# Sigmoid attention and a token mixer on one core: every transpose of q, k and x behind the first group in four 64x64 tiles

## The chip, the cores and the metric

The kernel runs on one core of one Trainium2 chip. The metric is the device time of one execution in microseconds. A core has five engines that run side by side and meet only through semaphores: TensorE (PE in the profile; its weight loads are shown apart as PEld), VectorE (DVE), ScalarE (ACT), GpSimd (POOL) and SyncE (SP), which here only issues DMAs. TensorE writes into PSUM, here eight banks of 2 KB for each of 128 partitions; another engine has to copy a result out of PSUM before the bank can be written anew.

## The reference

Inputs are q, k and v of shape (8, 12, 448, 64), and three weights, all f32; the output is (8, 448, 768) in f32.

```python
scores = q @ k.T / sqrt(64) - log(448)
attn   = sigmoid(scores)                    # no softmax: each element by itself
x      = (attn @ v), heads side by side     # (8, 448, 768)
wq, wk = x @ w_q, x @ w_k                   # 768 -> 64
W_tok  = wq @ wk.T / sqrt(64)               # 448 x 448 for each batch
out    = relu(W_tok @ x) @ w_out
```

The kernel computes W_tok @ x as wq @ (wk.T @ x), so the 448 x 448 matrix of the second part is never made.

## The kernel before, in words

**Work units.** Four heads of one batch are a group; there are 8 batches of 3 groups, 24 groups n = 0 to 23. Rows of a head are split as 448 = 7 x 64. For each group the kernel loads q, k and v (448 KB each, SP, L180) into one ring of five buffers, and POOL casts each to bf16 (L199). q and k have two cast buffers each, v three. A cast of q or k waits for the transposes of the group two before it, and a load waits for the cast that frees its ring buffer. So SP, POOL and PE are tied in a ring.

**Steps.** PE's work is written out by hand as a string of letters, PLAN (L125 to L152), and the loop at L649 turns each letter into one step, on all engines in that order:

- S: scores of one 64-row block, 4 matmuls of 64x64 tiles (L263) into a pair of banks, then one ACT sigmoid of 128x896 (L268). There are 168.
- P: attn @ v, 4 matmuls (L281). Seven P of a group add up in one pair of banks, which DVE copies out (L290).
- q and k, or a and b: transposes of one group's q or k (`tr`, L225). Letters q and k use `transposes`: 28 transposes of 64x64, in the four 64x64 tiles of the array (L213). Letters a and b use `transposes_whole`: 7 transposes of 128x128 in the whole array (L221). Both forms use one pair of banks for q and k together, and one DVE copy (L251 or L246).
- x or X: transposes of one group's part of x for the mixer (`tr_x`, L295). x: 32 transposes of 64x64 (L321), into a pair of banks. X: 8 of 128x128 (L304), into a single bank. One DVE copy follows either (L334 or L309).
- W, N, U, M: the steps of the mixer (L345, L361, L376, L399 or L411), and O: the output product (L481 for batches 0, 1, 6 and 7 in the whole array, L446 for the others in 64x64 tiles), with copies on DVE or ACT and stores from SP. Lower-case m, u and o put the copy on ACT.
- F: one matmul of zeros (L651).

The eight PSUM banks are four pairs, and they are handed out in the order in which they were released, as the program is built:

```python
    free2 = [0, 1, 2, 3]
    def bank2():
        n = free2.pop(0)
    def bank1():
        if halves:
            n, b = halves.pop(0)
        else:
            n, b = free2.pop(0), 0
            halves.append((n, 1))
```

`bank2` takes a pair, `bank1` a single bank: the free half of a pair that is already split, or the first half of a new one. `release` puts a pair at the end of the list. A step waits on PE until the copy of the step that had its banks before is done; the instructions behind it on PE wait too, since PE works in order. W keeps a single bank over six steps, P a pair over seven, and O a single bank or a pair over two or four.

In PLAN the first group's q and k are transposed ahead of the loop in the whole array (L631 to L641 and K), which stays so. Of the 23 pairs of q and k steps behind it, 11 are a and b (groups 1, 2, 4, 5, 7, 8, 9, 10, 13, 14 and 15); of the 24 x steps, 9 are X (groups 0, 1, 3, 4, 5, 6, 8, 10 and 16).

Of the kernel before, what the change touches and what calls it, by code (L numbers as in the profile page):

```python
# [16 lines left out]
def kernel(  # L17
# [94 lines left out]
    def xt(u, j):  # L112
# [11 lines left out]

    PLAN = (  # L125
        "FFFSSSFFFFFKFSSaFbSFSPPPP",
        "SSPPaPSbSSFqkSFFSFa",
        "SXSbSPPPPSPPFSPSabPSPPP",
        "SPPSPWWSXSxWSWWWSPPNSPPP",
        "SqPkSSPaSbSUSXSPPPM",  # L130
        "SPPPSPSabSaSbaSbSPPPMP",
        "SPPPSWXWSMSWXWSSWoWOSqkP",
        "SPPPSPPPSoOSSSoOONSO",
# [15 lines left out]
        "SUSoSoMOSOSPPPPxSPPPS",  # L149
        "PPPmPPMPPWWoWWWWoOxxNoOUOOoOMmMoOOoooOooOOOOooOooO",  # L150
    )
    PLAN = "".join(PLAN)  # L152
    KIND = ["a"] + [t for t in PLAN if t in "qac"]

    ld = {}
# [492 lines left out]

    for t in PLAN:  # L649
        if t == "F":  # L650
# [28 lines left out]
        elif kind == "M":  # L679
            u, x = divmod(c, NC // 2)  # L680
# [43 lines left out]
```

## Time and profile before

| | |
|---|---|
| timed runs, median of 3 | 204.12 us (203.43 to 205.49) |
| span of the profiled execution, first to last instruction | 200.3 us |
| PE busy | 187.9 us (94%), 3,948 matmuls and transposes |
| PEld busy | 122.1 us, 3,950 weight loads |
| ACT busy | 170.3 us (85%), of it 157.0 us the 168 sigmoids |
| DVE busy | 125.0 us (62%) |
| POOL busy | 82.1 us (41%) |
| DMA | 49.73 MB, mean 248 GB/s |
| granted TensorE clock, mean | 0.998 |

The profiled execution is one execution apart from the timed ones. Its records begin and end with its span, so no time around it can be read from it; the timed median lies 3.8 us above the span, and that difference is taken as fixed.

The page gives busy times, a picture of the span in 40 slices of 5 us, and the chain of work that ended last. Matmul records have modelled ends, which overlap the next start, so a busy PE can still hide short waits; how long a step holds PE is read from the start of its first matmul to the start of the next step's.

### The profile page before, as it was taken

The numbers are of one execution on the slowest core, as the hardware profiler recorded it, in microseconds if no ns is written. First come the engines' busy times: TensorE is split into PE (matmuls) and PEld (weight loads), VectorE is DVE, ScalarE is ACT, GpSimd is POOL, SyncE is SP. The second block draws the span as 40 slices with busy tenths as digits, with TensorE's granted clock in tenths as the row PEclk, the third lists the DMA queues.
The fourth block names the chain that finished last, engine by engine and source line by source line (L and its number), as shares of the span: only waits on it lengthen the run. The fifth ranks groups of instructions, "written<-read, shape, count | busy, mean of one in ns | idle before, by whom it ended". The sixth has DMA issues, their size and how long they took to land.

```text
span 200.3 us, 8999 instructions
## 1 busy us (share of the span) xinstructions
PE 187.9 (94%) x3948; PEld 122.1 (61%) x3950; DVE 125.0 (62%) x165; ACT 170.3 (85%) x194; POOL 82.1 (41%) x101
## 2 busy tenths in 40 slices
PE   8995998898999999999999999999999999999990
PEld 7452564455455655665557667778678869665560
DVE  3234375667755877846786856667787774774520
ACT  4798899798989999999889799999899989975520
POOL 2467777677677647558136320305061110000000
PEclk9999999999999999999999999999999999999999
DMA  5999999999999999899999983388704443332575
GB/s 174 317 351 374 292 361 324 357 358 322 356 352 348 367 389 315 293 320 339 285 318 352 338 301 104 86 242 208 256 17 99 105 109 81 84 79 49 142 211 154
DMA packets 29799, 49.73 MB, mean 248 GB/s; under 512 B 3904, under 2 KB 26560, under 8 KB 29760
## 3 DMA queue, kind: packets, MB, share of 16 engines
q1 hardware_dynamic: 29040, 47.78, 74.2%
q10 hardware_dynamic: 720, 1.38, 1.9%
q8 instruction: 31, 0.51, 1.0%
q14 instruction: 8, 0.07, 0.1%
HBM read 38.14 MB, written 11.01 MB: 245 GB/s over the span
## 4 chain that ended last, share of the span: by engine, by line
PE 61%; DMA 26%; POOL 5%; ACT 2%; issue 1%; SPq 1%; ACTq 1%; DVE 1%; POOLq 0%; DVEq 0%
PE banks L446 14%; PE banks L263 12%; PE banks L281 11%; PE banks L481 8%; DMA k<-in_k_dram 8%; DMA q<-in_q_dram 8%; DMA v<-in_v_dram 6%; DMA out_dram<-o 5%; PE banks L345 4%; POOL q L199 2%; PE banks L376 2%; PE banks L221 2%; PE banks L321 2%; PE banks L213 2%; ACT at L268 2%
## 5 line engine op out<-in xcount | busy, mean ns | idle before, releaser
L268 ACT ACTIVATE at<-banks,bias_t 128x896 bf16<-128x896 f32 x168 | 157.0, 1012 | 11.8 <-PE banks L263 9.5
L263 PE MATMUL banks<-qk 64*64 64x448 bf16 x672 | 62.4, 360 | 1.2 <-ACT at L268 0.5
L281 PE MATMUL banks<-at,v 64*64 64x448 bf16 x672 | 45.9, 350 | 0.5 <-issue 0.5
L263 PEld LDWEIGHTS <-qk 64*64 64x64 bf16 x672 | 24.9, 105 | 21.2 <-issue 13.7
L446 PE MATMUL banks<-wout,mx 64*64 64x384 bf16 x672 | 36.3, 323 | 0.0
L199 POOL CAST v<-v 128x896 bf16<-128x896 f32 x24 | 22.4, 933 | 30.5 <-PE banks L281 21.1
L290 DVE CAST xt<-banks 128x896 bf16<-128x896 f32 x23 | 25.1, 1090 | 12.6 <-PE banks L281 12.6
L481 PE MATMUL banks<-wout,mx 128*128 128x384 bf16 (+1 forms) x174 | 31.1, 321 | 0.0
L199 POOL CAST k<-k 128x896 bf16<-128x896 f32 x23 | 21.4, 932 | 18.2 <-PE banks L213 10.5
L281 PEld LDWEIGHTS <-v 64*64 64x64 bf16 x672 | 23.1, 106 | 6.6 <-issue 0.3
L387 DVE TENSOR_SCALAR mx<-banks 128x1024 bf16<-128x1024 f32 (+2 forms) x22 | 22.7, 1044 | 6.9 <-PE banks L411 3.5
L199 POOL CAST q<-q 128x896 bf16<-128x896 f32 x23 | 21.4, 932 | 9.3 <-DMA q<-in_q_dram 5.6
L446 PEld LDWEIGHTS <-mx 64*64 64x64 bf16 x672 | 22.6, 107 | 4.0
L481 PEld LDWEIGHTS <-mx 128*128 128x128 bf16 x174 | 15.6, 98 | 12.4 <-issue 3.8
L251 DVE COPY qk<-banks 128x1792 bf16<-128x1792 bf16 x12 | 13.1, 1090 | 8.7 <-PE banks L213 7.2
L511 DVE COPY o<-banks 128x384 f32<-128x384 f32 x18 | 10.0, 556 | 9.1 <-PE banks L481 8.6
L246 DVE COPY qk<-banks 128x1792 bf16<-128x1792 bf16 x11 | 12.0, 1091 | 5.5 <-PE banks L221 5.3
L455 DVE COPY o<-banks 128x768 f32<-128x768 f32 x14 | 13.4, 955 | 2.4 <-PE banks L446 2.3
L334 DVE COPY xn<-banks 128x1024 bf16<-128x1024 bf16 (+1 forms) x15 | 9.7, 654 | 5.3 <-PE banks L321 5.2
L345 PE MATMUL banks<-xt,wqk 128*128 128x448 bf16 x48 | 12.6, 354 | 0.3 <-DVE o L511 0.3
L603 POOL CAST wout<-w 128x768 bf16<-128x768 f32 x12 | 9.9, 827 | 5.8 <-DMA w<-in_moe_w_out_dram 5.6
L511 ACT COPY o<-banks 128x384 f32<-128x384 f32 x9 | 4.4, 484 | 7.7 <-PE banks L481 6.9
(60 smaller groups left out, 158.5 us busy)
## 6 DMA issues: line engine op xcount, KB each, us to landing
q<-in_q_dram SPq DMA_DIRECT2D x24, 448.0 KB, 5.8
v<-in_v_dram SPq DMA_DIRECT2D x24, 448.0 KB, 5.3
k<-in_k_dram SPq DMA_DIRECT2D x23, 448.0 KB, 6.0
out_dram<-o SPq DMA_DIRECT2D x48, 192.0 KB, 3.2
w<-in_moe_w_out_dram SPq DMA_DIRECT2D x11, 384.0 KB, 4.8
out_dram<-o ACTq DMA_DIRECT2D x6, 192.0 KB, 3.2
w<-in_moe_w_out_dram SPq DMA_DIRECT2D x2, 192.0 KB, 6.0
k<-in_k_dram SPq DMA_DIRECT2D x1, 256.0 KB, 5.2
```

The source lines that it names most:

```text
L199: eng.tensor_copy(out=t16.rearrange("p i b d -> p b i d"), in_=ld.pop((nm, n)).rearrange("p b (i d) -> p b i d", i=NI),)
L251: nc.vector.tensor_copy(out=qk[n].rearrange("p t h i n -> p t h (i n)"), in_=ps[:, :, 0 : 2 * S].rearrange("p h (t x) -> p t h x", t=2),)
L263: nc.tensor.matmul(sc[HALF[h], g, 0:S], qk[n][HALF[g], 1, h, i, :], qk[n][HALF[g], 0, h].rearrange("p i n -> p (i n)"), start=True, stop=True,
L268: nc.scalar.activation(at, sc[:, :, 0:S], ACTF.Sigmoid, bias=bias_t, scale=attn_scale)
L281: nc.tensor.matmul(ps[HALF[g], h, 0:S], ld["v16", n][HALF[h], i, g, :], ats[n, i][HALF[h], g, :], start=(i == 0), stop=(i == NI - 1),)
L290: nc.vector.tensor_copy(out=xt(u, j)[:, :, 0:S], in_=ps[:, :, 0:S])
L345: nc.tensor.matmul(ps, wqk16[:, c, :], xt(u, c // 2)[:, c % 2, 0:S], start=(c == 0), stop=(c == NC - 1),)
L387: nc.vector.tensor_scalar(dst, ps, moe_scale, 0.0, ALU.mult, ALU.max)
L446: nc.tensor.matmul(ps[HALF[x], y, 0:NB], mx[HALF[y], u, b, 64 * (i - 3 * y) : 64 * (i - 3 * y) + 64], wout16[HALF[y], slot(y, b), x * NB : ...
L455: COPY["s" if act else "v"](out=o, in_=ps[:, :, 0:NB])
L481: nc.tensor.matmul(ps, mxs[w][:, 2 * S * c + m * P : 2 * S * c + (m + 1) * P], wout16[:, c, w0:w1], start=(c == 0), stop=(c == NC - 1),)
L511: COPY["s" if act else "v"](out=o[:, nb * NB : (nb + 1) * NB], in_=ps)
```

## The change

One line is added behind the plan: each a becomes q, each b becomes k and each X becomes x. The sequence of steps is the same.

```diff
-    PLAN = "".join(PLAN)
+    PLAN = "".join(PLAN).replace("a", "q").replace("b", "k").replace("X", "x")
     KIND = ["a"] + [t for t in PLAN if t in "qac"]
```

KIND is used only to find a letter c, which occurs in neither plan. What a step does follows from its letter, in `tr`:

```python
        if kind in "ab":
            transposes_whole(ps[:, t], t16, slice(0, NI))
        else:
            transposes(ps[:, :, t * S : (t + 1) * S], t16, slice(0, NI))
```

and in `tr_x`, which for X takes `bank1()` and 8 whole transposes, and otherwise `bank2()` and four times 8 transposes of 64x64. PE's program grows from 7,902 to 9,258 instructions (28 transposes in place of 7 for a q or a k, 32 in place of 8 for an x, each with its weight load). On DVE the copies L246 and L309 become L251 and L334, one for one. ACT, POOL and SP have the same instructions in the same order.

## The prediction

> **What bounds the kernel now.** First the page: the busy slices and the chain.
>
> ```profile
> PE   8995998898999999999999999999999999999990
> ...
> ACT  4798899798989999999889799999899989975520
> ...
> DMA  5999999999999999899999983388704443332575
> ...
> PE 61%; DMA 26%; POOL 5%; ACT 2%; issue 1%; SPq 1%; ACTq 1%; DVE 1%; POOLq 0%; DVEq 0%
> ```
>
> PE ends the chain most, yet the DMA engines stand at 9 for the first 24 slices, and ACT is at 8 or 9 until 175 us. So I ask for busy times by stretch (start:end length, then PE, PEld, DVE, ACT, POOL, clock, DMA share, GB/s).
>
> ```profile
> 20.00:55.00 35.00, 32.15 (x567) 19.17 (x567) 22.68 (x26) 32.24 (x36) 25.89 (x32) 1.00 0.99 338
> 55.00:66.00 11.00, 10.68 (x204) 5.62 (x204) 6.38 (x10) 9.92 (x12) 8.15 (x11) 1.00 1.01 353
> 66.00:82.00 16.00, 15.97 (x304) 9.89 (x301) 12.86 (x15) 15.57 (x17) 8.70 (x10) 1.00 0.99 349
> 82.00:100.00 18.00, 17.72 (x392) 10.44 (x380) 11.82 (x16) 17.17 (x20) 10.66 (x12) 1.00 0.94 311
> ```
>
> Up to 55 us the loads set the pace: DMA share 0.99, and PE waits for casts that waited for a load, last 0.66 us at 55.29 for group 11's k. From 66 to 82 us PE has no idle time, but ACT has 0.43 us in 16: two bounds within 3%. Behind 142 us DMA is at 0.39 and PE is busy throughout.
>
> Which steps change where, from PE's timeline: eight of the 11 pairs stand before 47 us, the others at 66.0, 68.9 and 78.4; the X at 20.9, 28.8, 38.9, 49.7, 51.3, 74.1, 87.5, 99.0 and 142.8.
>
> **What a step costs PE.** The timeline has both forms (start, length, instruction).
>
> ```profile
> 63.22 0.38 PE L263 MATMUL banks<-qk 64*64 64x448 bf16 x4
> 63.43 0.39 PE L213 MATMUL banks<-ident,q 64*64 64x64 bf16 x28
> 63.65 0.43 PE L213 MATMUL banks<-ident,k 64*64 64x64 bf16 x28
> 63.91 0.38 PE L263 MATMUL banks<-qk 64*64 64x448 bf16 x4
> ...
> 68.63 0.36 PE L263 MATMUL banks<-qk 64*64 64x448 bf16 x4
> 68.93 0.56 PE L221 MATMUL banks<-ident,q 128*128 128x128 bf16 x7
> 69.33 0.55 PE L221 MATMUL banks<-ident,k 128*128 128x128 bf16 x7
> 69.81 0.38 PE L263 MATMUL banks<-qk 64*64 64x448 bf16 x4
> ```
>
> Read starts: 28 small transposes take 0.22 us, 7 whole ones 0.40 (68.93 to 69.33). Where the array changes form there is more: S takes 0.19 us before a step of its own form and 0.31 before a whole one (+0.12); the second whole seven takes 0.49 (+0.09). So a pair between S steps falls by 2 x 0.18 + 0.21 = 0.57 us. An X goes from 0.445 (8 whole, groups of the trace) to about 0.26 (32 small); between two W, which are whole, it loses the gain to two new changes of form (0.445 to 0.475). Sum: 22 x 0.18 + 9 x 0.185 = 5.6 us, and 11 fewer visits to the whole form x 0.21 = 2.4: PE sheds **8.0 us**, 6.2 of them before 55 us.
>
> [...]
>
> **Part 1, before 55 us: 0 (-0.4 to 0).** Faster PE work does not bring the next load sooner. The cover is the load stream; the DMA share leaves at most 3% of the ten busiest us before 50, some 0.3 us. PE merely waits longer for the same casts. The four stretches in which PE waits there (0.7 at 33.9, 1.0 at 35.8, 1.2 from 41.6 to 45.7, 0.8 at 54.2) also absorb what parts 3 and 5 cost this early.
>
> **Part 2, 55 to 74 us: -0.2 (-0.5 to 0).** Two pairs save 1.15 us on PE, but ACT takes only what it idles: 0.15 us at 65.8 and 0.21 at 73.47. S steps here start 0.09 to 0.5 us after their banks come free, so PE runs into ACT instead.
>
> **Part 3, other banks for x.** X fits into the free half of W's pair; x takes a whole pair, the oldest released. I followed the list of free pairs through both plans: 38 steps get other banks. Look at the X at 74.14.
>
> ```profile
> 72.98 0.57 PE L263 MATMUL banks<-qk 64*64 64x448 bf16 x8
> ...
> 73.77 0.54 PE L345 MATMUL banks<-xt,wqk 128*128 128x448 bf16 x2
> 74.14 0.61 PE L304 MATMUL banks<-ident,xt 128*128 128x128 bf16 x8
> 74.68 0.38 PE L263 MATMUL banks<-qk 64*64 64x448 bf16 x4
> 75.00 0.93 PE L345 MATMUL banks<-xt,wqk 128*128 128x448 bf16 x4
> ...
> 73.47 2.80 ACT L268 ACTIVATE at<-banks,bias_t 128x896 bf16<-128x896 f32 x3 [0.21 <-PE banks L263]
> ```
>
> At 72.98 PE issues S 67 and S 68; ACT runs them from 73.47 to 75.4. Before, the next S (69) took a pair free since 74.48. After, x waits for sigmoid 67 (74.48 instead of 74.14) and S 69 for sigmoid 68: 75.4 instead of 74.68. From an S to its sigmoid it is 0.49 us (72.98 to 73.47), so ACT stands idle 0.55 us, and, as four W (0.86) and a change of form stand between S 69 and S 70, another 0.2. **+0.8 us** (0.4 to 0.8; ACT has nothing in reserve there). The pair saved at 78.4 returns none: S 74 started 0.12 us after its bank came free. The X at 87.5 costs nothing: an O copy fills ACT (0.48 at 88.68). At 99.0 an S then waits for x's own DVE copy: **+0.2** (0 to 0.25). At 142.8 x waits for the DVE copy of P, which ends at 143.09: 0.37 + 0.26 + a form change of 0.12 against 0.445, **+0.3** (0 to 0.4). The cases at 28.8, 49.7 and 51.3 (up to 0.7 us) are in part 1's cover; without it they would cost 1.2.
>
> **Part 4, DVE: 0.** L246 and L251 take 1091 and 1090 ns, L309 and L334 688 and 690.
>
> **Part 5, more instructions: +0.5 (0 to 3).** The code itself comes by DMA.
>
> ```profile
> q8 instruction: 31, 0.51, 1.0%
> ...
> 113.51 0.57 PE L281 MATMUL banks<-at,v 64*64 64x448 bf16 x7
> 114.57 0.35 PE L281 MATMUL banks<-at,v 64*64 64x448 bf16 x1 [0.49 <-issue]
> ```
>
> 31 packets for 7,898 PE records: one packet is 255 instructions, and the records between packets agree. At 113.51 PE stops amid a step, one matmul short, for no semaphore; the packet records show one packet from 112.01 to 112.98, and the count there is a multiple of 256 if PE's sequencer runs 73 ahead. With that offset, the sequencer's entry into a block is followed by the end of the next block's packet after 1.7 to 5.2 us until 120 us (median 3.6), and after 1.3 to 3.1 later; first use was at least 1.1 us behind that end, and 1.6 where PE stopped. So while the DMA engines are full a block of 256 should last about 5 us. Before, blocks there last 4.8 to 9.4. A tiled pair has 112 instructions in 0.45 us, and with the new counts laid on the old times blocks shrink to 4.2 to 4.7 for most of 21 to 49 us, and to 3.7, 4.1, 3.5 and 4.5 at 63.0, 66.7, 78.4 and 87.8. The early ones are in part 1's cover. Of the late four I take 0.5 us in all: none if the short delays hold (1.7 and 2.4 at 57 and 73), 3 if the long ones do (3.6 to 4.4 at 80 to 91).
>
> [...]
>
> **Sum:** 0 - 0.2 + 0.8 + 0.2 + 0.3 + 0 + 0.5 = +1.6 us on the span of 200.3; with the 3.8 us between span and median, 204.12 + 1.6 = **205.7 us**.
>
> **Rivals.**
>
> *PE's saving comes through* (faster). It does if the loads have slack and ACT's gaps close: ACT idles 3.7 us from 20 to 60 and 0.7 us from 60 to 90; half of the first and most of the second give about -2.5 us, 201.6. For it: the chain names PE most, and the DMA rate reaches 389 GB/s in one slice against 338 here. Against: casts wait for loads up to 55 us. It decides whether group 11's k (cast at 54.30) comes over 1.5 us sooner.
>
> *Code comes too late* (slower). Place: the blocks at 63.0 to 92 us; price up to 1 us each, plus early ones beyond the 3.8 us cover; it decides if crossing to use exceeds 4.5 us in them. +4, 208.
>
> *Everything is hidden:* PE's lead swallows part 3 and part 5, 204.1. For it: PE waits 3.8 us before 55. Against: ACT is at 97% where part 3 falls.
>
> That the tiled transposes do not run at 7.8 ns beside full DMA is not a rival: 12 pairs already do, at 17.7, 54.2 and 63.4 too.
>
> **Chances.** Forecast 0.50 (204.4 to 207.0), code late 0.18 (207 to 210), hidden 0.18 (203.6 to 204.4), saving 0.14 (199 to 203.3). About 1% (2 us) is what a measurement of this kernel can tell, with 203.43 to 205.49 for one kernel. Over 206.16 lie all of the second and a third of the first: slower 0.34; under 202.08 about 0.09; within 1% 0.57. Range 202.3 to 208.4: a third of the saving and some half of the late code are in, and what is left out is under 2 in 10.
>
> **What would show it.** Right: 0.22 us from q to k at all pairs; k 11 cast within 0.5 us of 54.3; an ACT idle of about 0.5 us before S 69; ACT at 97% around 66 to 82. Late code: PE idle on "issue" in mid-step, and 36 or 37 packets on q8. Wrong: sigmoids 1 us or more ahead by 55 us, or PE idle of several us at x steps.

## The result, and the profile after

The changed kernel takes 212.28 us (median of 3, 211.28 to 214.16) against 204.12: a ratio of 1.041 (95% interval 1.031 to 1.052). The forecast was 205.7 with a range of 202.3 to 208.4. It is slower, by more than the range allows. The rival that came true is the one of the code that comes too late, but it cost 8.2 us where I gave it 4, and the time lies above that rival's own 207 to 210 too.

The profiled execution after has a span of 210.5 us. Later runs list each execution's span beside its time, and the time lies 1.8 to 1.9 us above the span, not 3.8: the profiled execution of before, at 200.3, was 2 us faster than its own median. In what follows the two traces are compared span with span (+10.2 us), and times with times (+8.2 us).

The page of the changed kernel, the same slices (with the clock) and the chain:

```profile
PE   7968869776799978999899999999989999999991
...
ACT  4796979895699978999787989999969899994521
...
PEclk9997999996999999999999999999999999999998
DMA  6999999999999999369996896457823333530585
...
PE 75%; issue 7%; ACT 6%; DMA 6%; DVE 1%; ACTq 1%; POOL 1%; SPq 1%; DVEq 0%
...
q8 instruction: 36, 0.59, 1.1%
```

"issue", time in which PE waited for nothing that the profile shows, went from 1% to 7% of the chain; DMA went from 26% to 6%. PE is less busy in the first 16 slices, and the granted clock has slices at 7 and 6. Five more packets of code were loaded, 36.

Busy time by stretch, after, with the columns of the prediction (stretch and its length in us; PE with its matmul records in brackets, weight loads, DVE, ACT, POOL; granted clock; DMA share; GB/s):

```profile
20.00:55.00 35.00, 26.36 (x816) 16.95 (x812) 18.31 (x20) 28.15 (x30) 24.27 (x29) 0.93 1.00 330
55.00:66.00 11.00, 10.69 (x226) 6.03 (x222) 7.30 (x9) 9.86 (x11) 7.75 (x9) 1.00 0.99 348
66.00:82.00 16.00, 13.83 (x357) 7.54 (x356) 10.47 (x13) 13.94 (x16) 9.09 (x10) 1.00 0.99 337
82.00:100.00 18.00, 17.25 (x459) 10.01 (x443) 12.15 (x16) 17.05 (x20) 8.40 (x10) 1.00 0.71 245
```

From 20 to 55 us PE is busy for 26.4 us and ACT for 28.2, where both had 32.2 before; from 66 to 82 PE fell from 16.0 to 13.8 and ACT from 15.6 to 13.9. Not only PE: all that follows PE got less work in the same time.

What PE's idle time waited for, before (cause: us in total, times, longest), two lines of the table of waits of PE alone:

```profile
PE banks L263 <- ACT at L268: 0.5, 1, 0.5
PE banks L281 <- issue: 0.5, 1, 0.5
```

and after:

```profile
PE banks L263 <- issue: 4.0, 3, 2.2
PE banks L213 <- issue: 2.6, 3, 1.6
PE banks L263 <- ACT at L268: 2.5, 7, 0.5
PE banks L281 <- issue: 1.7, 2, 1.0
...
PE banks L321 <- ACT at L268: 1.3, 4, 0.5
...
PE banks L321 <- issue: 0.9, 1, 0.9
PE banks L481 <- issue: 0.8, 1, 0.8
```

Idle on "issue" rose from 0.5 to 10.0 us over ten stops, on five kinds of line: it is no step of its own that is slow. Waiting for ACT, that is for banks, rose from 0.5 to 3.8.

PE's timeline at the largest stop, after:

```profile
46.67 0.38 PE L263 MATMUL banks<-qk 64*64 64x448 bf16 x3 [0.30 <-ACT at L268]
49.29 0.53 PE L263 MATMUL banks<-qk 64*64 64x448 bf16 x1 [2.24 <-issue]
49.29 0.74 PE L213 MATMUL banks<-ident,k 64*64 64x64 bf16 x25
```

S is four matmuls; three are issued at 46.67 and the fourth 2.6 us later, with no semaphore between them. Count PE's records, and add 73 as in the prediction. Of the gaps of over 0.45 us between two neighbours, ten then sit where the count is 7 modulo 256, in blocks 2, 4, 6, 7, 8, 9, 12, 13, 17 and 28: 12.8 us from start to start. So a block of code is 256 of PE's records in this trace. I call these stops at a block's end. At each of them the packet of the next block had ended 1.2 to 1.6 us before PE went on. The trace of before has one such stop, of 0.8 us at 113.7, the one that the prediction shows; a gap of 0.5 us at 18.5 has nearly the same count, but the last packet had ended 5.3 us before it was over.

How late each S step starts after against before gives the course of the loss (us, by the number of the S step):

| S step | start before | later after | what stands there |
|---|---|---|---|
| 18 | 24.2 | 0.5 | |
| 21 | 26.8 | 1.9 | stop at 25.7 |
| 39 | 44.2 | 2.5 | stops at 36.4 and 41.8, partly caught up |
| 48 | 54.0 | 6.4 | stops at 46.7 and 53.3 |
| 51 | 57.4 | 5.4 | wait for group 11's cast, shorter than before |
| 66 | 71.6 | 7.0 | stop at 76.4 |
| 69 | 74.7 | 7.9 | bank waits at x and S |
| 90 | 95.3 | 8.9 | stop at 100.6 |
| 138 | 145.1 | 9.2 | bank wait at x |
| 141 | 148.6 | 10.2 | stop at 155.1 |
| 165 | 173.9 | 10.2 | |

Not all of the 5.4 us up to 57 us need be the change's. The run with only the last three pairs changed (below) has the code of before up to 60 us, and no stop at a block's end there; in its trace S 51 starts 2.7 us later than in the trace of before all the same, since casts and loads came later.

The steps themselves cost what was forecast. PE's timeline of the pair of group 12, after, and then the case that was priced bank by bank, S 67 to S 69:

```profile
60.40 0.38 PE L263 MATMUL banks<-qk 64*64 64x448 bf16 x4
60.61 0.39 PE L213 MATMUL banks<-ident,q 64*64 64x64 bf16 x28
60.83 0.43 PE L213 MATMUL banks<-ident,k 64*64 64x64 bf16 x28
...
80.14 0.57 PE L263 MATMUL banks<-qk 64*64 64x448 bf16 x8
...
81.69 0.45 PE L321 MATMUL banks<-ident,xt 64*64 64x64 bf16 x32 [0.23 <-ACT at L268]
82.59 0.38 PE L263 MATMUL banks<-qk 64*64 64x448 bf16 x4 [0.45 <-ACT at L268]
```

From 60.61 to 60.83, 0.22 us for 28, some 7.8 ns each. And both x and S 69 wait for ACT.

### The profile page after: what moved, and what is told of

It reads as the page before. It is cut to its first block, busy times and chain, and to the rows that moved or that the text cites. A ratio compares the mean times of both kernels' runs of the same rounds, so it can differ in the third digit from the quotient of the medians.

```text
span 210.5 us, 10363 instructions
## 1 busy us (share of the span) xinstructions
PE 187.6 (89%) x4628; PEld 121.5 (58%) x4628; DVE 125.5 (60%) x165; ACT 171.2 (81%) x194; POOL 81.8 (39%) x101
## 4 chain that ended last, share of the span: by engine, by line
PE 75%; issue 7%; ACT 6%; DMA 6%; DVE 1%; ACTq 1%; POOL 1%; SPq 1%; DVEq 0%
PE banks L263 16%; PE banks L281 14%; PE banks L446 13%; PE banks L481 13%; ACT at L268 6%; PE banks L213 4%; PE banks L345 4%; PE banks L321 4%; DMA q<-in_q_dram 3%; DMA k<-in_k_dram 3%; PE banks L376 3%; PE banks L399 1%; DVE xt L290 1%; ACTq L490 1%; PE banks L651 1%
## 5 line engine op out<-in xcount | busy, mean ns | idle before, releaser
L268 ACT ACTIVATE at<-banks,bias_t 128x896 bf16<-128x896 f32 x168 | 157.9, 1008 | 21.3 <-PE banks L263 18.5
L263 PE MATMUL banks<-qk 64*64 64x448 bf16 x672 | 65.6, 364 | 7.2 <-issue 4.0
L281 PE MATMUL banks<-at,v 64*64 64x448 bf16 x672 | 47.4, 353 | 1.7 <-issue 1.7
L263 PEld LDWEIGHTS <-qk 64*64 64x64 bf16 x672 | 26.7, 106 | 23.3 <-issue 17.7
L251 DVE COPY qk<-banks 128x1792 bf16<-128x1792 bf16 x23 | 25.1, 1090 | 14.7 <-PE banks L213 14.7
L281 PEld LDWEIGHTS <-v 64*64 64x64 bf16 x672 | 24.6, 107 | 8.4 <-issue 3.2
L334 DVE COPY xn<-banks 128x1024 bf16<-128x1024 bf16 (+1 forms) x24 | 16.0, 669 | 11.6 <-PE banks L321 10.6
L321 PEld LDWEIGHTS <-xt 64*64 64x64 bf16 x768 | 10.7, 109 | 6.9 <-issue 6.4
L213 PEld LDWEIGHTS <-q 64*64 64x64 bf16 x644 | 9.6, 112 | 6.7 <-issue 3.5
L321 PE MATMUL banks<-ident,xt 64*64 64x64 bf16 x768 | 11.2, 194 | 2.6 <-ACT at L268 1.3
L213 PE MATMUL banks<-ident,q 64*64 64x64 bf16 x644 | 10.1, 198 | 3.3 <-issue 1.6
```

Of the source, the lines that this page charges most:

```text
L213: nc.tensor.transpose(ps[HALF[g], h, x * NP : (x + 1) * NP], t16[HALF[h], i, g, :], ident16[HALF[h], HALF[h]],)
L251: nc.vector.tensor_copy(out=qk[n].rearrange("p t h i n -> p t h (i n)"), in_=ps[:, :, 0 : 2 * S].rearrange("p h (t x) -> p t h x", t=2),)
L263: nc.tensor.matmul(sc[HALF[h], g, 0:S], qk[n][HALF[g], 1, h, i, :], qk[n][HALF[g], 0, h].rearrange("p i n -> p (i n)"), start=True, stop=True,
L268: nc.scalar.activation(at, sc[:, :, 0:S], ACTF.Sigmoid, bias=bias_t, scale=attn_scale)
L281: nc.tensor.matmul(ps[HALF[g], h, 0:S], ld["v16", n][HALF[h], i, g, :], ats[n, i][HALF[h], g, :], start=(i == 0), stop=(i == NI - 1),)
L321: nc.tensor.transpose(ps[HALF[c], g, (2 * m + h) * HD : (2 * m + h + 1) * HD], xt(u, j)[HALF[g], h, (2 * m + c) * HD : (2 * m + c + 1) * H ...
```

## The experiments

Two theories stand against each other, and a third beside them. **Theory 1:** PE's code comes in blocks of 256 instructions, each one DMA packet of 16,384 bytes (36 for 9,256 records of PE after, 31 for 7,898 before), and while the loads fill the DMA engines (share 0.99 to 1.00 from 20 to 82 us) the packet comes later than PE is through with a block with two tiled pairs in it. In the trace after, 34 of the 36 packets start 0.1 to 4.2 us after PE's first record in the block ahead, and the last two 0.7 and 1.3 us before it; what asks for a packet was not shown. **Theory 2:** the pairs of banks that x now takes. **Theory 3:** the split array itself, or the lower clock.

### Only q and k; only x; only the banks; and half as many transposes

Four kernels on the same chip; the kernel before had a median of 204.56 there. The first two take one half of the change each:

```diff
-    PLAN = "".join(PLAN)
+    PLAN = "".join(PLAN).replace("a", "q").replace("b", "k")      # only q and k
+    PLAN = "".join(PLAN).replace("X", "x")                        # only x
```

> Only the 22 a and b steps become q and k; the nine X stay in the whole array and keep their banks. PE's program has 924 instructions more than before, against 1,356 in the changed kernel. Theory 1 (code comes too late: while the DMA engines are full, PE gets a block of 256 instructions only every 5 to 6 us): stops of PE in mid-step, all at the same place modulo 256, 4 to 8 us of them before 60 us; the time is 208.5 to 211. Theory 2 (the x steps' pairs of banks are the cost): within 1 us of before, or up to 2 us faster, since the saving on q and k remains. Theory 3 (small transposes are slow beside full DMA, or the clock falls): 28 of them take clearly more than 0.22 us, time as in the changed kernel in proportion to 11 of 11 pairs, 210 or more.

Measured: 210.03 us, ratio 1.030 (1.023 to 1.037). Seven stops at a block's end, 8.7 us, of it 4.6 from 25 to 51 us. One of them, PE's timeline:

```profile
48.34 0.28 PE L213 MATMUL banks<-ident,k 64*64 64x64 bf16 x11
51.17 0.32 PE L213 MATMUL banks<-ident,k 64*64 64x64 bf16 x17 [2.55 <-issue]
```

Eleven of the 28 transposes of one k, and the rest 2.8 us later. Most of the loss comes without any change of banks: theory 2 can't be the main cause.

> Only the nine X become x; a and b stay whole. 432 instructions more than before, spread over 20 to 143 us. Theory 1: one to three stops in mid-step, 0.5 to 1 us each, and the bank waits that the prediction priced at 1.3 us (0.8 at S 69, 0.2 near 100 us, 0.3 near 143 us): together 205.5 to 207. Theory 2 says that all of the loss is here: 210 or more.

Measured: 210.18, ratio 1.031 (1.023 to 1.038), the five times from 205.4 to 211.0. More than expected, and scattered: the two lowest, 205.4 and 208.3, are only 0.4 and 1.8% above the median of before. The profile was of the fastest (span 203.6); it has two stops at a block's end, at 85.1 and 118.4, 2.3 us. (The 3.5 us in the next expectation include two gaps that are no such stops: one behind a matmul of zeros at 19.6, one in which PE waits for a cast of k at 46.5.) S 69 waits as priced: it loses 0.75 us against the steps before it. As the rest was open, the same kernel ran once more:

> The kernel with only the nine X changed, once more, since its first five runs lay between 205.4 and 211.0 us with the profile taken of the fastest. If code stops vary from run to run (theory 1), the times scatter again over several us, and a profile of a slower run shows more of its loss in stops at the block's end than the 3.5 us of the first; the bank wait of 0.75 us at S 69 is in every profile. If something else makes it slow, the stops stay at 3.5 us and the loss sits elsewhere.

Measured: 209.41, ratio 1.024 (1.017 to 1.031), 207.4 to 213.0. The profile has a span of 208.2 and four stops at a block's end, 4.7 us. Three of them lie where nothing was changed, one on an S before W:

```profile
120.32 0.38 PE L263 MATMUL banks<-qk 64*64 64x448 bf16 x3
122.13 0.35 PE L263 MATMUL banks<-qk 64*64 64x448 bf16 x1 [1.43 <-issue]
```

Two more of that kind are at 141.0 (1.2 us, in a P) and 151.8 (0.9, in an O). The instructions added ahead of them, up to 432, put the ends of all later blocks elsewhere in the code. So the x half is also code, beside 1.0 to 1.3 us of bank waits. Its scatter from run to run agrees with that, but only two of nine executions were profiled.

The banks alone, with the whole transposes kept:

```diff
-            fb, _, ps = bank1()
-            ps = ps.rearrange(...)
+            fb, _, ps = bank2()
+            ps = ps[:, 0].rearrange(...)
```

> The kernel before, but X takes a pair of banks as x does, and still does its 8 transposes in the whole array. No instruction is added. This measures the bank waits alone. The prediction's price: S 69 0.7 to 0.8 us later, 0.2 near 100 us, up to 0.4 near 143 us, 1.3 us in all, 205.4; no new stop in mid-step. Theory 2: most of the 8 us, 209 or more. If the early waits at 28.8, 49.7 and 51.3 us are not hidden: 206.5.

Measured: 206.51, ratio 1.010 (1.003 to 1.018): +2.0 us (the interval is 0.6 to 3.6), near the case in which the early waits are not hidden. But the trace says otherwise: its timelines, PE and then ACT, around S 69,

```profile
74.75 0.61 PE L304 MATMUL banks<-ident,xt 128*128 128x128 bf16 x8 [0.23 <-ACT at L268]
75.64 0.38 PE L263 MATMUL banks<-qk 64*64 64x448 bf16 x4 [0.29 <-ACT at L268]
...
73.69 1.91 ACT L268 ACTIVATE at<-banks,bias_t 128x896 bf16<-128x896 f32 x2 [0.21 <-PE banks L263]
76.13 2.13 ACT L268 ACTIVATE at<-banks,bias_t 128x896 bf16<-128x896 f32 x2 [0.54 <-PE banks L263]
```

show the 0.54 us of idle ACT that was forecast as 0.55, and S 69 loses 0.75. The early waits cost S 24 to S 48 up to 1.5 us, and by S 51 1.0 of it is caught up. Near 100 and 145 us the S steps lose 0.24 and 0.29. Beyond these 1.3 us the trace has code: a stop at a block's end at 86.7 (2.1 us in this execution) and one of 0.7 near 100, in place of that at 113.7 before. Not one PE instruction was added here, so where the stops fall also depends on how the times happen to lie.

Fourth, everything small made twice as wide: 64 rows by 128 columns, half the instructions, the same banks and copies.

```diff
-            for g in range(2):
-                for h in range(2):
-                    nc.tensor.transpose(
-                        ps[HALF[g], h, x * NP : (x + 1) * NP], t16[HALF[h], i, g, :],
+            for h in range(2):
+                nc.tensor.transpose(
+                    ps[:, h, x * NP : (x + 1) * NP], t16[HALF[h], i].rearrange("p b d -> p (b d)"),
+                    ...
```

(and the same for x).

> The changed kernel with every small transpose twice as wide: 64 rows by 128 columns of the array, so 14 transposes for a q or k and 16 for an x in place of 28 and 32. The same results land in the same banks, the same copies follow; PE's program has 9,258 - 23 x 2 x 28 - 24 x 32 = 7,202 instructions, 700 fewer than before. Theory 1: no stops in mid-step or one; what is left of the changed kernel is the bank waits (1.3 us) less some PE time: 203 to 205.5. Theories 2 and 3: as slow as the changed kernel, 210 to 213, as the banks are the same and the array is still split.

Measured: 206.90, ratio 1.015 (1.007 to 1.022). Of the 4.1% of the change, 2.6 are gone, with the same banks. No stop at a block's end is left in its trace (span 206.7). The time is above the expected range: besides the bank waits (0.75 at S 69 again), S steps lose 0.13 to 0.2 us at many of the late groups. A q takes 0.20 us, but a change between this form and that of S costs some 0.1 us each way, at every step: S holds PE for 0.32 us before a q (66.24) in place of 0.19 before a step of its own form, and k for 0.30 before an S (66.77) in place of 0.20.

### The same array, the length of the code of before

The kernel with only q and k changed, with 7 of each 28 transposes left in:

```diff
             for g in range(2):
                 for h in range(2):
+                    if few and 4 * x + 2 * g + h > 6:
+                        continue
+                    ...
```

> The kernel with the 22 a and b steps as small transposes in four tiles, but only the first 7 of the 28 are done (the copy repeats one block for all seven, so three quarters of the transposing is left out); X stays whole. PE's program has exactly the length of the kernel before, 7,902, and the array's form, the banks and the copies are those of the run with only q and k changed, which took 210.0. Theory 1 (code comes too late): the 4 to 8 us of stops go, 202.5 to 205. Theory 3 (the split array, the clock, or the change of form): stays at 208 to 210, as 21 small transposes of 8 ns (0.16 us a step, 3.6 us of PE's time in all, most of it where PE waits for loads) can't explain 5.5 us.

Measured: 205.00, ratio 1.006 (0.999 to 1.014), against 1.030 with all 28. The 21 transposes left out are 0.16 us of PE's time in a step, and they are worth some 5 us over the kernel. Theory 3 falls with it, the clock too: the mean clocks of its compared executions are 0.973 to 0.988, no higher than the changed kernel's 0.978 to 0.987, and it is 5 us faster. (The result is not the kernel's: three quarters of these transposes are missing, and the copy repeats one block in their place.)

The traced execution is the slowest of ten, 208.3 us. It has no stop at a block's end before 87 us, and then three, at 87.3, 93.7 and 125.2, 3.3 us in all. The largest, PE's timeline:

```profile
93.30 0.68 PE L369 MATMUL banks<-xn,wkn 128*64 128x384 bf16 x5
95.95 0.48 PE L369 MATMUL banks<-xn,wkn 128*64 128x384 bf16 x3 [1.97 <-issue]
```

There the packet started 5.6 us after PE had entered the block ahead. So single packets can come late in a program as long as that of before, too.

### Half of the load traffic

Only half of each load is brought, and the cast reads that half twice, so the results are not the kernel's:

```diff
         eng.dma_start(
-            out=t,
-            in_=SRC[nm][u, 4 * j : 4 * j + 4].rearrange(...),
+            out=t[:, 0],
+            in_=SRC[nm][u, 4 * j : 4 * j + 4].rearrange(...)[:, 0],
```

> The changed kernel, but each load of q, k and v behind the first group brings only half of the bytes (the other half of each buffer is left unread, the cast reads the loaded half twice). Instructions of PE, forms and banks are those of the changed kernel. Theory 1: the code's packets no longer stand behind full DMA queues, so the stops shrink to less than 2 us in all, and as loads no longer set the pace either, the time falls below that of the kernel before: 190 to 198, and no more than 2 us above the kernel before with the same half loads; it may even be faster than that one, as PE sheds 8 us. Theory 3 or the banks alone: 5 us or more above the kernel before with half loads.

> The kernel before with the same half loads of q, k and v, as the measure for the changed kernel with half loads. Loads set the pace up to 55 us, so both theories expect it faster than before: 193 to 200, with ACT's idle time between 20 and 60 us (3.7 us) mostly gone.

Measured: 200.99 after and 197.10 before, ratios of 0.986 (0.978 to 0.994) and 0.968 (0.959 to 0.976) to the full kernel before. The gap between the two is 3.9 us in place of 8.2, and the stops fall from 12.8 to 1.9 us, two in number. From entering a block (PE's first record in it) to the start of the next block's packet, the median over the first 100 us is 1.5 us with half loads and 3.1 with full ones; in the kernel before it is 0.8 and 2.1. The DMA share by stretch, changed kernel with half loads:

```profile
20.00:55.00 35.00, 31.27 (x943) 19.03 (x935) 23.56 (x27) 33.30 (x37) 26.95 (x34) 1.00 0.77 232
```

The 3.9 us are more than theory 1 expected (2 at most). By the starts of the S steps, bank waits make up about 2.8 of them (0.6 by S 27, about 0.8 by S 48, 0.75 at S 69, 0.4 near 100 us, 0.2 near 145; the early ones have no cover here) and two stops at block ends (45.9 and 143.8) about 1.2. That PE's 8 us bring nothing even here fits the prediction's view that ACT takes the saving: from 20 to 55 us ACT is busy for 33.3 of the 35 us in this trace, PE for 31.3, and the loads' share is 0.77.

### Only the last three pairs

```diff
+        late.append(dict(a="q", b="k")[t] if t in "ab" and seen[t] > 8 else t)
```

> Only the last three pairs (groups 13, 14 and 15, at 66, 69 and 78 us) become q and k; 252 instructions more. PE sheds 1.7 us where ACT is at 97%. Theory 1: one or two stops in mid-step between 66 and 125 us, 0.5 to 1.5 us each, little gained: 204 to 206.5. If instead the loss sits in the first 55 us alone: 202.5 to 204.3.

Measured: 204.64, ratio 0.997 (0.990 to 1.004) to before. The change of three pairs is neither gain nor loss that could be measured. The loss of the q and k half sits with the eight pairs before 47 us, and with what their instructions move.

The traced execution, 207.95 and the slowest of ten, has three stops at a block's end in the stretch named, at 83.2, 89.0 and 114.0, 3.7 us in all; the largest:

```profile
88.47 0.86 PE L270 MATMUL banks<-qk 64*64 64x448 bf16 x11
91.06 0.35 PE L270 MATMUL banks<-qk 64*64 64x448 bf16 x1 [1.73 <-issue]
```

So the stops were there in this execution, one more than expected. How many stops the quicker executions had, or those of the kernel before, which took 200.7 to 208.0 us on this chip, was not seen.

### 48 instructions that do nothing

If only the place of a block's end counts, then shifting it without any change of work must cost time too.

```diff
+            if done["S"] == 12 and done["q"] == 3:
+                for _ in range(24):
+                    nc.tensor.matmul(
+                        pairs[free2[0]][HALF[0], 0, 0:1], zeros[HALF[0], 0:64], zeros[HALF[0], 0:1],
+                        ...
```

> The kernel before with 48 PE instructions more (24 weight loads and matmuls of one column of zeros, into a free bank), put where PE idles 1.4 us before group 3's q at 17.7 us. No other work, form, bank or order changes; only the ends of the 256-instruction blocks behind that point fall 48 instructions earlier in the code. Theory 1: with the new ends laid on the old trace, the blocks that end at 83.3, 112.5 and 146.1 us last 3.1, 4.0 and 3.0 us where about 5 (DMA full) and 3.6 are wanted, so stops of 1 to 2 us at 83, of 0.5 to 1.5 near 112 (in place of the 0.7 at 113.5), and up to 0.6 at 146: 1 to 3 us slower than before, ratio 1.005 to 1.015. If the number or place of the blocks does not matter: no change, below 1.003.

Measured: 205.44 against 205.09 of before on that chip, ratio 1.005 (1.001 to 1.009): slower by a little, just below the size expected. The places are as named. The trace runs 2.4 and 3.1 us later than the old one there, so 83.3 becomes 85.7 and 112.5 becomes 115.6:

```profile
85.69 0.55 PE L281 MATMUL banks<-at,v 64*64 64x448 bf16 x7
86.96 0.54 PE L281 MATMUL banks<-at,v 64*64 64x448 bf16 x5 [0.72 <-issue]
...
115.44 0.68 PE L446 MATMUL banks<-wout,mx 64*64 64x384 bf16 x11
117.30 0.32 PE L446 MATMUL banks<-wout,mx 64*64 64x384 bf16 x1 [1.17 <-issue]
```

Stops of 1.1 and 1.5 us from start to start, and none at 146 or at the old place in the code of the stop at 113.7. This trace also has a stop of another kind, 3.2 us at 36 us for a cast that waited for group 7's k: a load that came late, which is no matter of code.

### A version with fewer instructions than before

The wide form is cheaper than the whole one between S steps (0.63 against 1.01 us a pair) and has half the instructions of four tiles. With x and X as before, and q and k wide up to group 19:

```diff
-        if kind in "ab":
-            transposes_whole(ps[:, t], t16, slice(0, NI))
-        else:
+        if n < 20:                       # the other version: n < 24
+            transposes_wide(ps[:, :, t * S : (t + 1) * S], t16, slice(0, NI))
+        else:
```

> x and X as before; the transposes of q and k of groups 1 to 19 as 14 of 64 rows by 128 columns of the array, those of groups 20 to 23 in four 64x64 tiles as before. PE's program has 7,762 instructions, 140 fewer than before. By the run with everything in this form a pair takes 0.41 us and two changes of form (0.21), against 1.01 whole and 0.44 in four tiles: PE sheds 11 x 0.38 - 8 x 0.2 = 2.6 us, and the 8 pairs that were in four tiles issue half the instructions. Theory 1: no bank waits and fewer stops than before, 0.5 to 2 us faster than before, 202 to 204, less spread from run to run; but ACT at 97% and the loads may hide all of it. Theory 3 (splitting the array costs by itself): slower than before by 1 us or more.

Measured: 206.63, ratio 1.013 (1.008 to 1.018): slower, where faster was expected.

> The same with all 23 pairs of q and k in 64 by 128. 7,538 instructions, 364 fewer than before. Against the version with groups 20 to 23 in four tiles PE pays 4 x 0.2 us more, behind 127 us where PE sets the pace: 0.8 us slower than that one, unless a stop between 127 and 160 us goes for it.

Measured: 204.24, ratio 0.999 (0.995 to 1.003): as before, and better than the version above, against the expectation. The profile of the first has stops at 108.5, 137.7 and 169.9 (3.0 us), two of them beyond the stretch of full DMA; the second has none. Near 100 us the first also waits 1.1 us for a copy o on DVE that waited for a store of the output, which is no code. PE shed 2.6 us by the estimate in the first, and it shows nowhere. So no version here with the right result beats the kernel before.

## Why the prediction was wrong

**What failed is part 5 and the cover that part 1 lent it.** Part 5 said "+0.5 us (0 to 3)" for late code and put the early short blocks "in part 1's cover". Measured in the trace after: 12.8 us of stops, 8.3 of them between 15 and 55 us. The mechanism had been named; the term was mis-sized, and the cover did not hold.

1. *The delay was taken from a kernel that did not press it.* I worked with 5 us from entry to use (3.6 and some 1.3). In the eight stops of the trace after up to 80 us, PE started again 3.8 to 6.5 us after it entered the block, six times over 5.3. The packet's end was followed by PE's start after 1.24 to 1.61 us in all ten stops, and the packet itself took 0.9 to 1.3, once 2.1. What grew is the time to its start, a median of 3.1 us after against 2.1 before, over the first 100 us. And one trace does not give the longest delay: the run with 7 of 28 transposes had a packet start 5.6 us late, where the trace of before has 3.2 at most.
2. *The blocks were laid on old times.* Old times contain old waits and the slower whole transposes. Without the stop itself, the five blocks ahead of the stops from 25.7 to 53.3 lasted 3.9 to 4.6 us, a little less than the 4.2 to 4.7 that I read off. This is the smaller error: with the delay, 4.9 to 6.5 us there, it made each stop 0.8 to 2.6 us and not some tenths.
3. *The cover was counted twice.* Part 1 counted 3.8 us of PE's waits for loads before 55 us (its four stretches add up to 3.7) as cover for bank waits and for code. Stops of 7.6 us from 25.7 to 53.3 alone exceed it. And the cover moves: a stopped PE transposes later, the next cast and load start later, so group 11's k was cast at 56.5 instead of 54.3.
4. *The late blocks were the right ones, at too low a price, and one was overlooked.* Of the four that I named on the old times, those at 63.0, 66.7 and 87.8 did end in stops, now at 71.8, 76.4 and 100.6, 3.3 us in all where I took 0.5; the one at 78.4 did not, its packet having started only 0.1 us after the entry. The stop at 155.1, 1.1 us, lies behind all that I looked at. The 1,356 instructions had shifted the block ends there too, and that a stretch with unchanged steps can lose time by this was not in the prediction. Much of the surprise with only x changed is of this kind.

**The rival had the mechanism right and the point of decision nearly so** ("if crossing to use exceeds 4.5 us"), but its price, 208, and its chance, 0.18, came from the same delay.

**What held.** The cost of the transposes: 0.22 us for 28 (0.218 in the trace after too). Part 2: PE's 8 us brought nothing, not even with half the loads. Part 3: S 69 lost 0.75 to 0.87 us in six traces (forecast 0.8), ACT idled 0.54 us (0.55); near 145 us the S step lost 0.23 to 0.43 in four (0.3). The early bank waits, which I put at 1.2 us without cover, cost 1.4 with half loads. Part 4: the copies take 1,090 and 691 ns on average (1,090 and 690). Part 1 held as to the saving; it failed as to the cover. (PE's saving adds up to 7.9 us and not 8.0, as 11 times 0.21 is 2.3; nothing hangs on it.) The tell-tale named for late code, PE idle on "issue" amid a step and 36 or 37 packets, came as named: 36.

**What stays open.** Where a packet of code waits, behind full DMA queues as theory 1 has it or elsewhere, was not measured, only that its start comes later with more load traffic (3.1 against 1.5 us) and, at the same traffic, in the changed kernel than in the one before (3.1 against 2.1, 1.5 against 0.8). The 73 of the count is a fitted number: the traces don't tell a sequencer that runs ahead from instructions that leave no record. The granted clock was 0.50 from 18.2 to 21.6 and from 48.9 to 52.3 us. The second stretch began within the stop at 46.7; behind it 25 small transposes took 0.52 us (49.29 to 49.81) and 28 took 0.40 (50.57 to 50.97) where 28 take 0.22. Behind the stops at 25.7, 36.4 and 41.8, and from the one at 53.3 to 209.3 us, the clock stayed at 1.00. If PE does half the work in a stretch at half the clock, two stretches of 3.4 us cost it 3.4 us together at most (an estimate from these figures). The clock's share in the loss was not measured alone; with 7 of 28 transposes the mean clock was no higher and the time 5 us better, so it is no main term.

## What to carry to other kernels

Count instructions as a resource with a rate: here, at the stops, PE got 256 per 3.8 to 6.5 us while loads filled the DMA engines and per 4.0 us at the late stop (155.1), so a form that does the same work with four times the instructions can lose although each is faster and PE's own time falls. Look for gaps in mid-step without a semaphore, at a fixed count modulo the block, and move or thin the dense stretch that sits there; a cheaper form with fewer instructions (64 by 128 instead of 64 by 64) took most of the loss away. Instructions added or left out shift the block ends behind them, so a small difference between two versions of a kernel can come from code that the edit didn't touch: 48 idle instructions brought stops at 85.7 and 115.4 us and cost 0.5% (0.1 to 0.9).

## What the runs showed of the hardware

- At a stop at a block's end, PE went on 1.24 to 1.61 us after the end of the block's packet of 16,384 bytes (all ten stops of the trace after), whatever the line; in the other traces it was 1.0 to 1.6.
- The packet starts 3.1 us (median, first 100 us) after PE enters the block ahead while loads run in full and 1.5 with half loads, in the kernel before 2.1 and 0.8; behind 125 us it is 1.1 in the trace after, with a DMA share of 0.60 up to 142 us and 0.46 from there to 178.
- 14 transposes of 64 rows by 128 columns take 0.20 us, about as little as 28 of 64 by 64 (0.22) and half of 7 whole ones (0.40); a change between this form and 64 by 64 costs about 0.1 us each way (0.32 against 0.19, 0.30 against 0.20).
- 48 idle instructions in a place where PE waits anyway cost 0.5% (0.1 to 0.9).
